# Attention block on one core: reordered first loads, and a reworked last stage

## The chip, the cores and the metric

The kernel runs on one core of one Trainium2 chip. The metric is device time in microseconds (us) of one execution. Each kernel was executed several times; where two kernels are compared, their executions alternated on the same chip. A profile shows one execution; its "span" is about 1.8 us shorter than the time of the same execution (841.5 against 843.27 us for the kernel before).

## The reference, cut to what matters

```python
def setup_inputs():
    B, Sq, D = 8, 208, 1024
    H, Sk, Dh = 32, 1024, 128          # all tensors bf16
    # x (B,Sq,D), k_cache and v_cache (B,H,Sk,Dh), wq (D,H*Dh), wo (H*Dh,D)

def reference(x, k_cache, v_cache, wq, wo):
    q = (x @ wq).reshape(B, Sq, H, Dh).transpose(0, 2, 1, 3)
    scores = einsum("bhqd,bhkd->bhqk", q, k_cache) * (Dh ** -0.5)
    p = softmax(scores, axis=-1)
    o = einsum("bhqk,bhkd->bhqd", p, v_cache)
    return o.transpose(0, 2, 1, 3).reshape(B, Sq, H * Dh) @ wo
```

K and V are 67 MB each and are read once. The weights are 8.4 MB each, x is 3.4 MB.

## The kernel before

The work is cut into 32 blocks: 4 groups of 8 heads, and in each group the 8 batches. A block needs K of its 8 heads (2 MB, transposed on the way in by the DMA), V (two chunks of 1 MB), its group's wq (two halves of 1 MB) and wo (2 MB), and x transposed. TensorE works through the heads one by one: scores, the exponential on ScalarE, the product with V, the row sum, and between them the q projection of a later block and output projections of the block before.

The first loads, in the order in which they are issued (DMAs of `nc.sync` are issued by SyncE, SP in the profile, on its hardware queue; those of `nc.gpsimd` by GpSimd, POOL, on the software queue):

```python
    load_wq_half(0, 0)                                        # POOL, 1 MB
    nc.sync.dma_start_transpose(out=xT[:, :, :Sq], in_=xf[:Sq, :])      # x of batch 0
    ...
    kv_of[0] = load_kv(*blocks[0], first=True)

    def load_kv(g, b, first=False):
        ...
            if first and ck == 0 and hck > 2:                 # K of heads 0 and 1 first, 0.5 MB
                nc.sync.dma_start_transpose(out=kT_c[:, :2 * Sk], in_=k_cache[b, h0:h0 + 2]...)
            else:                                             # K of all 8 heads, 2 MB
                nc.sync.dma_start_transpose(out=kT_c[:], in_=k_cache[b, h0:h0 + hck]...)
        for ck in range(NCKV):                                # two chunks of V
            ...
            nc.sync.dma_start(out=v_c[:], in_=v_cache[...]...)
            if first and ck == 0:
                load_wq_half(g, 1)                            # POOL, 1 MB
                load_wo(g)                                    # POOL, 2 MB
                nc.sync.dma_start_transpose(out=kts[0][:, 2 * Sk:], ...)   # K of heads 2 to 7, 1.5 MB
                nc.sync.dma_start_transpose(out=xT[:, :, Sq:], in_=xf[Sq:, :])  # x of batches 1 to 7, 3 MB
```

The output projection, as the last group runs it. Its one buffer in PSUM, the memory that TensorE writes to, is `po`; VectorE empties it (below called the eviction):

```python
    ps_p = ctx.enter_context(tc.tile_pool(name="f_ps_p", bufs=1, space=PSUM))
    ...
                po = ps_p.tile([128, 512], F32, name="po")
                for hl in range(hg):                          # 8 matmuls of 128x512
                    nc.tensor.matmul(po[...], lhsT=oT[:, hl, r0:r0 + rows], rhs=wo_g[:, hl, ...], ...)
                ...
                    nc.vector.tensor_tensor(out=o_sb[:rows, :], in0=po[:rows, :CW], in1=a, op=ALU.add)
                    nc.vector.reduce_sum(out=fin[...], in_=o_sb[:rows, :], axis=AX.X)
                    nc.sync.dma_start(out=of[...], in_=o_sb[:rows, :])
```

At the end VectorE (DVE) checks sums that were collected (`chk`, `chk_hi`, `fin`) and makes a flag; the flag goes to DRAM by a DMA, every engine loads it into a register, and branches over a slow safe version that is not needed here:

```python
        ...                                                   # 4 compares, 5 reductions, a cast
        nc.tensor.matmul(cnt[0:1, 0:1], lhsT=ok_bf[:], rhs=ones[:], start=True, stop=True)
        nc.vector.tensor_scalar(out=bad[:], in0=cnt[0:1, 0:1], scalar1=127.5, scalar2=None, op0=ALU.is_lt)
        nc.vector.tensor_copy(out=bad_i[:], in_=bad[:])
        nc.sync.dma_start(out=flag_d[:], in_=bad_i[:])
    cond = nc.values_load(flag_d[0:1, 0:1], min_val=0, max_val=1)
    with tc.If(cond > 0):
        mha_slow(tc, x, k_cache, v_cache, wq, wo, out)
```

## Time and profile before

The median was 841.38 us in four runs.

Busy time by stretch, from the windows view of the kernel before. The columns are the stretch in us from the start, its length, the busy time of PE (TensorE matmuls), PEld (weight loads), DVE, ACT and POOL with the number of instructions, the TensorE clock that was granted, the DMA share and the rate in GB/s.

```profile
10.00:20.00 10.00, 4.92 (x31) 3.84 (x29) 1.18 (x2) 0.00 (x0) 0.00 (x0) 0.92 1.08 312
20.00:30.00 10.00, 4.67 (x35) 4.46 (x36) 1.62 (x5) 2.91 (x4) 0.00 (x0) 0.57 1.16 202
30.00:40.00 10.00, 6.76 (x70) 5.98 (x68) 5.37 (x16) 5.52 (x12) 0.00 (x0) 1.00 1.25 236
...
500.00:600.00 100.00, 97.39 (x923) 83.86 (x928) 76.30 (x238) 75.41 (x164) 1.77 (x2) 1.00 0.73 188
```

In the middle (last row) PE is busy 97% of the time and the DMA has room, 0.73. In the head it is the other way round: the DMA is full and PE is half idle.

What PE waited for in the head, from the waits view of the kernel before (engine, tile and line, what it waited for, us in total, times, the longest):

```profile
PE s_ps L316 <- DMA kT_c<-in_k_cache_dram: 14.2, 3, 9.7
PE q L271 <- DMA wq_g<-in_wq_dram: 9.6, 1, 9.6
PE q L271 <- DMA xT_all<-in_x_dram: 3.0, 1, 3.0
```

The three waits for K are those for the heads 0 and 1 (9.7 us, the scores start at 25.3 us), for heads 2 to 7 (2.8 us, at 33.5) and for block 1 (1.6 us, at 58.8).

The DMA view explains the 25.3 us. The first three lines are the stretch from 10 to 18 us, the next three that from 18 to 25 us. GB/s comes in 40 slices; q0 is the software queue (wq half 1 and wo), q1 the hardware queue (here K of heads 0 and 1, by transpose).

```profile
GB/s 175 197 248 390 283 285 283 285 288 421 476 390 326 328 328 376 563 369 306 326 349 398 498 367 305 349 415 480 388 312 324 369 440 476 312 323 317 387 297 337
q0 software_dynamic: 654, 2.58, 82.8%
q1 hardware_dynamic: 911, 0.23, 18.9%
...
GB/s 233 196 197 168 165 165 145 121 117 108 92 80 80 123 67 50 45 45 45 50 48 56 63 51 78 73 60 37 60 37 107 37 48 25 37 48 37 64 138 351
q1 hardware_dynamic: 841, 0.35, 111.4%
q0 software_dynamic: 84, 0.31, 10.8%
```

Until 18 us the software queue moved 2.58 MB and the transpose of K 0.23 MB.

The tail, from the timeline of the kernel before (start, duration, engine, line, operation, tiles, and in brackets the idle time before it and what ended it):

```profile
821.04 0.38 DVE L359 TENSOR_TENSOR oT<-o_ps,rinv 128x208 bf16<-128x208 f32 x1 [0.96 <-ACT rinv L352]
...
822.65 1.89 PE L287 MATMUL po<-wo_g,oT 128*128 128x512 bf16 x8 [0.78 <-DVE o_sb L302]
824.57 0.69 DVE L302 TENSOR_TENSOR o_sb<-po,acc 128x512 bf16<-128x512 f32 x1 [1.26 <-PE po L287]
825.30 0.69 DVE L304 TENSOR_REDUCE fin<-o_sb 128x1 f32<-128x512 bf16 x1
825.32 1.89 PE L287 MATMUL po<-wo_g,oT 128*128 128x512 bf16 x8 [0.78 <-DVE o_sb L302]
...
833.63 0.14 DVE L533 CAST bad_i<-bad 1x1 int32<-1x1 f32 x1
833.84 0.30 SPq L535 DMA_DIRECT2D flag_d<-bad_i  x1
```

The last head is done at 821.4 us. Then PE and DVE take turns at the one PSUM buffer, and the program ends 20.1 us later, at 841.5.

### The profile page before, as it was taken

To read this page: it belongs to the slowest core of one execution; us is meant where nothing else is said; L and a number is where in the kernel's file an instruction comes from. 1 tells how busy PE (TensorE), PEld (TensorE's weight loads), DVE (VectorE), ACT (ScalarE), POOL (GpSimd) and SP (SyncE) were. 2 spreads that over 40 slices of the span, in tenths; PEclk is the share of its full clock that TensorE was granted. 3 is DMA by queue.
4 is the path that set the end of the run, shared out by engine and by line. 5 is a ranking of instruction groups with operands and counts; after the bars stand their busy time and mean duration, and the time that the engine had idled before them with its cause. 6 is when DMAs were issued, how large, how long until landed. Compare 5 with 4: busy or idle time off the path is not lost.

```text
span 841.5 us, 18460 instructions
## 1 busy us (share of the span) xinstructions
PE 776.6 (92%) x7180; PEld 658.5 (78%) x7233; DVE 623.0 (74%) x1889; ACT 590.1 (70%) x1281; POOL 10.9 (1%) x16
## 2 busy tenths in 40 slices
PE   2679999999999999999999999999999999999983
PEld 2578788888878888888788888788888888888861
DVE  0458777778777777777777777777877888888883
ACT  0448677768767778767677877676877867777770
POOL 1000000000000000000000000000000000000000
PEclk9899999999999999999999999999999999999998
DMA  9999686868779787559969957768867986876500
GB/s 239 232 287 230 176 193 162 198 152 241 179 200 249 183 183 197 135 142 248 228 173 226 231 123 193 182 156 238 216 166 230 216 219 166 213 179 175 150 26 29
DMA packets 318497, 159.08 MB, mean 189 GB/s; under 512 B 278210, under 2 KB 281538, under 8 KB 318402
## 3 DMA queue, kind: packets, MB, share of 16 engines
q1 hardware_dynamic: 314114, 141.04, 69.8%
q0 software_dynamic: 4288, 16.78, 6.0%
q8 instruction: 58, 0.95, 0.5%
q14 instruction: 37, 0.30, 0.1%
HBM read 83.89 MB, written 3.41 MB: 104 GB/s over the span
## 4 chain that ended last, share of the span: by engine, by line
PE 51%; DVE 24%; ACT 14%; SPq 5%; issue 3%; DMA 2%; DVEq 0%
PE po L287 21%; DVE t L338 14%; ACT pT L319 13%; PE o_ps L329 11%; PE q L271 10%; PE s_ps L316 9%; DVE oT L359 3%; DVE qT_gb L215 3%; DVE t1c L342 2%; SPq L253 2%; DMA kT_c<-in_k_cache_dram 2%; SPq L255 1%; SPq L240 1%; PE o_ps L348 1%; ACT rinv L352 1%
## 5 line engine op out<-in xcount | busy, mean ns | idle before, releaser
L319 ACT ACTIVATE pT<-s_ps 128x832 bf16<-128x832 f32 x512 | 415.0, 859 | 220.0 <-PE s_ps L316 215.9
L271 PE MATMUL q<-xT_all,wq_g 128*128 128x208 bf16 x2048 | 248.2, 255 | 18.0 <-DMA wq_g<-in_wq_dram 9.6
L316 PE MATMUL s_ps<-qT_gb,kT_c 128*128 128x208 bf16 x2048 | 244.9, 254 | 14.4 <-DMA kT_c<-in_k_cache_dram 14.2
L329 PE MATMUL o_ps<-pT,v_c 128*128 128x208 bf16 x2048 | 241.9, 253 | 14.9 <-DVE oT L359 7.9
L316 PEld LDWEIGHTS <-kT_c 128*128 128x128 bf16 x2048 | 209.6, 144 | 35.1 <-DMA kT_c<-in_k_cache_dram 14.9
L271 PEld LDWEIGHTS <-wq_g 128*128 128x128 bf16 x2048 | 188.9, 99 | 26.5 <-issue 13.3
L329 PEld LDWEIGHTS <-v_c 128*128 128x128 bf16 x2048 | 182.9, 97 | 32.1 <-issue 25.0
L287 PE MATMUL po<-wo_g,oT 128*128 128x512 bf16 x779 | 191.0, 380 | 6.0 <-DVE o_sb L302 2.3
L338 DVE TENSOR_TENSOR t<-pT 128x832 bf16<-128x832 bf16 x256 | 151.6, 592 | 49.3 <-ACT pT L319 36.9
L338 DVE TENSOR_TENSOR t<-t 128x416 bf16<-128x416 bf16 (+1 forms) x512 | 161.8, 316 | 9.0
L342 DVE TENSOR_SCALAR_CACHE_REDUCE t1c<-t 128x208 bf16<-128x208 bf16 x256 | 94.7, 370 | 92.0 <-PE o_ps L348 71.5
L287 PEld LDWEIGHTS <-oT 128*128 128x128 bf16 x832 | 80.3, 98 | 77.3 <-issue 3.2
L352 ACT ACTIVATE rinv<-lnrs 128x208 f32<-128x208 f32 x256 | 97.2, 380 | 7.9
L350 ACT ACTIVATE lnrs<-o_ps 128x208 f32<-128x208 f32 x256 | 89.8, 351 | 2.3 <-PE o_ps L348 2.3
L215 DVE CAST qT_gb<-q 128x416 bf16<-128x416 f32 x128 | 75.1, 587 | 20.5 <-PE q L271 19.9
L359 DVE TENSOR_TENSOR oT<-o_ps,rinv 128x208 bf16<-128x208 f32 (+10 forms) x256 | 83.8, 328 | 2.0 <-ACT rinv L352 1.9
L348 PE MATMUL o_ps<-t1c,ones_bf 128*128 128x208 bf16 x256 | 64.7, 253 | 0.2
L299 DVE TENSOR_TENSOR acc<-po,acc 128x512 f32<-128x512 f32 x52 | 36.0, 692 | 17.1 <-PE po L287 17.1
L352 ACT ACTIVATION_READ_ACCUMULATOR rinv<-lnrs 128x1 f32 x256 | 48.0, 188 | 0.0
L302 DVE TENSOR_TENSOR o_sb<-po,acc 128x512 bf16<-128x512 f32 x26 | 18.0, 691 | 10.2 <-PE po L287 10.2
L348 PEld LDWEIGHTS <-ones_bf 128*128 128x128 bf16 x256 | 25.0, 98 | 0.0
L215 DVE COPY acc<-po 128x512 f32<-128x512 f32 x26 | 18.0, 693 | 8.3 <-PE po L287 8.3
(27 smaller groups left out, 76.5 us busy)
## 6 DMA issues: line engine op xcount, KB each, us to landing
v_c<-in_v_cache_dram SPq DMA_DIRECT2D x64, 1024.0 KB, 5.5
wq_g<-in_wq_dram POOLq DMA_DIRECT2D x8, 1024.0 KB, 8.3
wo_g<-in_wo_dram POOLq DMA_DIRECT2D x4, 2048.0 KB, 10.3
out_dram<-o_sb SPq DMA_DIRECT2D x26, 128.0 KB, 2.1
kT_c<-in_k_cache_dram SPq DMA_TRANSPOSE x33, 11.2
xT_all<-in_x_dram SPq DMA_TRANSPOSE x2, 10.2
flag_d<-bad_i SPq DMA_DIRECT2D x1, 0.0 KB
```

The lines of the kernel that those rows point to most:

```text
L215: nc.vector.tensor_copy(out=out_ap, in_=in_ap)
L271: nc.tensor.matmul(q2[:, j, :Sq], lhsT=wq_h[:, t, hw * 128:(hw + 1) * 128], rhs=xT[:, t, b * Sq:(b + 1) * Sq], start=(t == 0), stop=(t == ...
L287: nc.tensor.matmul(po[:rows, :CW], lhsT=oT[:, hl, r0:r0 + rows], rhs=wo_g[:, hl, c * CW:(c + 1) * CW], start=(hl == 0), stop=(hl == hg - 1))
L316: nc.tensor.matmul(s_ps[:, jj // npb, (jj % npb) * Sq:(jj % npb + 1) * Sq], lhsT=kv[:, t, :], rhs=qT_gb[:, hl, :], start=True, stop=True)
L319: nc.scalar.activation(out=pT[:, half * T2:(half + 1) * T2, :].rearrange("p (a b) s -> p a (b s)", a=2), in_=s_ps[:, :, :npb * Sq], func=A ...
L329: nc.tensor.matmul(o_ps[:, :Sq], lhsT=v_c[:, hh, t, :], rhs=pT[:, t, :], start=(t == 0), stop=(t == T - 1))
L338: nc.vector.tensor_tensor(out=nxt[:], in0=cur[:, :n2, :], in1=cur[:, n2:n, :], op=ALU.add)
L342: nc.vector.tensor_scalar(out=t1c[:], in0=cur, scalar1=T1_CLAMP, scalar2=None, op0=ALU.min, op1=ALU.max, accum_out=chk_hi[:, u["idx"]:u["i ...
L348: nc.tensor.matmul(o_ps[:, 256:256 + Sq], lhsT=ones_bf[:], rhs=u["t1"][:, 0, :], start=True, stop=True)
L350: nc.scalar.activation(out=lnrs[:], in_=o_ps[:, 256:256 + Sq], func=ACT.Ln)
L352: nc.scalar.activation(out=rinv[:], in_=lnrs[:], func=ACT.Exp, scale=-1.0, accum_out=chk[:, u["idx"]:u["idx"] + 1])
L359: nc.vector.tensor_tensor(out=oT[:, u["hl"], c0:c0 + n1], in0=u["o_ps"][:, :n1], in1=u["rinv"][:, :n1], op=ALU.mult)
```

## The change

It shortens the two ends. In the head, what is not needed for block 1's start moves back: x is transposed batch by batch, each a block ahead; wo is cut in halves, half 0 after the first block's V, half 1 after block 1's V; wq half 1 and the first wo halves go through SP instead of POOL. In the tail, the last four output projections take the score tiles' two PSUM buffers; the sum `fin` comes out of the eviction itself; there are fewer checks; and the flag is read from SBUF. Fewer checks also means a weaker one: the two compares of `fin` with a bound became one test that `fin` is finite.

```diff
-    def load_wq_half(g, half):
+    def load_wq_half(g, half, eng=None):
...
-        nc.gpsimd.dma_start(out=w[:], in_=wq[...]...)
+        (eng or nc.gpsimd).dma_start(out=w[:], in_=wq[...]...)
...
+    def load_xT(b0, b1):
+        nc.sync.dma_start_transpose(out=xT[:, :, b0 * Sq:b1 * Sq], in_=xf[b0 * Sq:b1 * Sq, :])
...
+        if g == 0 and not first and b + 1 < B:
+            load_xT(b + 1, b + 2)
         for ck in range(NCKV):
+            if first and ck == 0:
+                load_wq_half(g, 1, eng=nc.sync)
             v_c = ...
             if first and ck == 0:
-                load_wq_half(g, 1)
-                load_wo(g)
                 ... # K of heads 2 to 7
-                    nc.sync.dma_start_transpose(out=xT[:, :, Sq:], in_=xf[Sq:, :])
+                    load_xT(1, 2)
+            if first and ck == NCKV - 1:
+                load_wo(g, 0, eng=nc.sync)
+        if bi == 1:
+            for c in range(1, NC):
+                load_wo(g, c, eng=nc.sync)
...
+                if tail:
+                    po = ps_s.tile([128, 2, 512], F32, name="s_ps")[:, 0, :]
...
-                    nc.vector.tensor_tensor(out=o_sb[:rows, :], in0=po[:rows, :CW], in1=a, op=ALU.add)
-                    nc.vector.reduce_sum(out=fin[...], in_=o_sb[:rows, :], axis=AX.X)
+                        nc.vector.scalar_tensor_tensor(out=o_sb[:rows, :], in0=po[:rows, :CW], scalar=1.0, in1=a,
+                                                       op0=ALU.mult, op1=ALU.add, accum_out=fcol)
...
-        flag_d = dram.tile([1, 1], I32, name="flag_d")
-        nc.sync.dma_start(out=flag_d[:], in_=bad_i[:])
-    cond = nc.values_load(flag_d[0:1, 0:1], min_val=0, max_val=1)
+        cond = nc.values_load(bad_i[0:1, 0:1], min_val=0, max_val=1)
```

Left out: renamings, the checks, and a way to split the last projections by heads that is switched off (`HS = 0`).

## The prediction

> **What bounds the kernel now.** TensorE, except at both ends. In the windows view PE is busy about 97% from 60 to 800 us at granted clock 1.00; one block of eight heads takes about 24.5 us (spacing of the Ln activations in the timeline). The unused time is in the first 60 us (PE busy 31.6, DMA share above 1.0) and after about 813 us.
>
> Head (timeline and landings): K of the first two heads lands at 25.3 us (the scores wait 9.7 us for it), while wq half 1 and the 2 MB wo share the engines; K of heads 2-7 lands at 33.4 (2.8 us of wait), the 3 MB transposed x of batches 1-7 at 45.6 (3.0 us), K of block 1 at 58.75 (1.6 us). The Trainium skill, "DMA: Bandwidth & Descriptors", section "Issuing engines are not separate DMA queues", says that DMAs of all issuers interleave on the same 16 engines; the trace agrees: the software queue's wo landed at 24.9 us and the transpose only then.
>
> Tail: the last oT ends at 821.4; then output projections alternate with the DVE eviction, as there is one PSUM buffer (matmuls 1.9 us, eviction 0.69, PE waits 0.78 each), until 830.6; then fin 0.69, checks to 833.8, the flag's DMA to 834.9, register load 0.66, branch (3.5 us on PE) and end, 841.5.
>
> **What the change does.** Head: block 1's K now stands behind about 9.9 MB instead of 13.4 (six batches of x, wo half 1 and V move behind it). At the 228 GB/s of the old head that is 43 to 45 us. The first K should land near 11 us, heads 2-7 near 25; PE's block 0 work also fits into about 43 us. Against this, x of batch 2 and V of block 1 come after that K, by my estimate 2 to 3 us of new wait near 45-52 us. Net gain 12 us (9 to 14).
>
> Tail: two PSUM buffers and no reduction: the last eviction ends near 826.9 instead of 831.3 on the old clock, 4.4 us. Fewer checks: 0.55 us. The flag read from SBUF: about 1.07 us, its DMA. The branch stays. Last block with 0.69 us less DVE per piece: 0.5 to 1 us, as DVE is 90% busy there. Sum 6.5 to 7 us.
>
> Middle: nothing. The 26 removed reductions (18 us of DVE) are off the critical path: PE's matmuls per 100 us are the same in the last group (902) as in groups without reductions (904, 902). The wo halves and x loads by batch have slack.
>
> **Prediction.** 841.4 - 12 - 7 = 822.4 us, range 816 to 829. Faster by over 2% 0.64, same 0.35, slower 0.01. The 2% line is at 824.6, so the head's size decides.
>
> **What would show each step.** Landings: K of two heads before 13 us, of heads 2-7 at 23-28, of block 1 at 42-47. Ln of block 1's first head near 55 us instead of 67.0. Block length still 24.5 us. In the tail PE runs the last 16 output-projection matmuls almost without waits, no fin reduction, no flag DMA; about 14 us from last oT to the end instead of 20.
>
> **What would make it wrong.** Block 1 waits for x of batch 2 or V longer than 3 us; wq half 1 on SP delays V or K of heads 2-7; early blocks run short of K (new DMA waits at blocks 2 to 4); the eviction with accumulation is much slower than 0.69 us; the register load from SBUF is slower.

## More of the kernel before

Note the granted clock of 0.57 between 20 and 30 us; what PE does do there runs slowly.

From about 19 us on the rate lay between 25 and 123 GB/s for some five microseconds, although the engines were marked busy.

## The result, and the profile after

The changed kernel took 821.78 us (median of 10 runs, 821.08 to 822.73). The ratio to the kernel before is 0.9767, with a 95% interval of 0.9742 to 0.9791. A later set of runs, on another chip, gave 821.07 us and a ratio of 0.9772. The spread fell too: 1.65 us over those 10 runs, against 11 us over the 15 runs of before.

The windows of the changed kernel:

```profile
10.00:20.00 10.00, 7.99 (x76) 7.07 (x75) 4.09 (x10) 3.38 (x5) 0.00 (x0) 1.00 1.11 316
20.00:30.00 10.00, 6.82 (x72) 6.32 (x71) 5.05 (x16) 5.41 (x12) 0.00 (x0) 1.00 1.12 289
30.00:40.00 10.00, 9.68 (x104) 8.97 (x101) 7.07 (x22) 7.86 (x16) 0.00 (x0) 1.00 1.25 244
...
500.00:600.00 100.00, 97.46 (x911) 82.98 (x916) 75.93 (x234) 74.70 (x164) 1.76 (x2) 1.00 0.75 190
```

The DMA is as full as before, but PE gets 72 matmuls instead of 35 between 20 and 30 us, and at full clock. The middle is unchanged.

Its waits in the head. The 8.8 us for x are in truth the start: PE's first matmul needs x of batch 0 and the first half of wq, and both land at about 8.4 us.

```profile
PE q L281 <- DMA xT_all<-in_x_dram: 8.8, 2, 8.6
PE s_ps L335 <- DMA kT_c<-in_k_cache_dram: 2.7, 2, 2.5
PE o_ps L348 <- DMA v_c<-in_v_cache_dram: 1.3, 1, 1.3
PE po L304 <- DMA wo_g<-in_wo_dram: 1.3, 1, 1.3
```

The last line is new: block 1 waits for wo half 1.

The DMA view of 10 to 18 us, to be read beside that of the kernel before: the software queue (q0) is gone from it, and q1 alone moved 2.58 MB (wq half 1, V, then K of heads 2 to 7), where q0 and q1 together had moved 2.81.

```profile
GB/s 133 15 215 256 271 333 343 364 369 369 389 364 374 328 358 379 379 379 389 328 358 410 358 440 358 420 287 348 349 421 273 269 221 288 288 289 292 291 292 289
q1 hardware_dynamic: 3624, 2.58, 106.4%
```

Its tail, by the timeline:

```profile
804.90 0.38 DVE L378 TENSOR_TENSOR oT<-o_ps,rinv 128x208 bf16<-128x208 f32 x1 [1.00 <-ACT rinv L371]
805.76 0.69 DVE L315 SCALAR_TENSOR_TENSOR o_sb<-s_ps,acc 128x512 bf16<-128x512 f32 x1 [0.48 <-PE s_ps L304]
...
806.51 3.61 PE L304 MATMUL s_ps<-wo_g,oT 128*128 128x512 bf16 x16 [0.36 <-DVE o_sb L315]
...
810.16 0.69 DVE L315 SCALAR_TENSOR_TENSOR o_sb<-s_ps,acc 128x512 bf16<-128x512 f32 x1 [1.03 <-PE s_ps L304]
...
812.89 0.15 DVE L555 TENSOR_SCALAR bad_i<-cnt 1x1 int32<-1x1 f32 x1 [0.35 <-PE cnt L550]
```

The last 16 matmuls run as one piece, no separate reduction follows, and the program ends 14.1 us after the last head instead of 20.1.

For the head, three points of the trace say most. They are the starts of PE's scores of head 0, of head 2 and of block 1, with the Ln activation (ScalarE's logarithm of the row sum) of block 1's first head, after which the kernels run alike. In the profiled runs:

| us | scores head 0 | scores head 2 | scores block 1 | Ln block 1 | Ln of last block | last head done | end |
|---|---|---|---|---|---|---|---|
| before | 25.3 | 33.5 | 58.8 | 67.0 | 803.5 | 821.4 | 841.5 |
| after | 13.6 | 23.7 | 40.0 | 49.1 | 787.4 | 805.3 | 819.3 |

So the head gave 17.9 us in this pair, the middle took back 1.8 (738.3 against 736.5 us), the last block stayed at 17.9 us, and the tail gave 6.0. The sum is 22.2 us, 3.7 more than the medians differ (18.5). The profiled run of before took 843.27 us, 3.0 above its median, so its head was one of the slower ones; that is tested next.

### The profile page after: what moved, and what is told of

Its sections match the earlier page's. It is cut to its first block, busy times and chain, and to the rows that moved or that the text cites. A ratio compares the mean times of both kernels' runs of the same rounds, so it can differ in the third digit from the quotient of the medians. Undisturbed runs are those within 1.5% of the kernel's fastest.

```text
span 819.3 us, 18488 instructions
## 1 busy us (share of the span) xinstructions
PE 773.1 (94%) x7181; PEld 655.4 (80%) x7233; DVE 604.6 (74%) x1885; ACT 590.7 (72%) x1281; POOL 11.8 (1%) x17
## 4 chain that ended last, share of the span: by engine, by line
PE 53%; DVE 25%; ACT 14%; DMA 3%; issue 3%; SPq 1%; DVEq 0%
PE po L304 20%; DVE t L357 15%; ACT pT L338 13%; PE o_ps L348 12%; PE q L281 10%; PE s_ps L335 9%; DVE oT L378 4%; DVE qT_gb L215 3%; DVE t1c L361 2%; DMA kT_c<-in_k_cache_dram 2%; DMA wo_g<-in_wo_dram 1%; PE o_ps L367 1%; SPq L243 1%; PE s_ps L304 1%; ACT rinv L371 1%
## 5 line engine op out<-in xcount | busy, mean ns | idle before, releaser
L281 PE MATMUL q<-xT_all,wq_g 128*128 128x208 bf16 x2048 | 245.6, 254 | 14.2 <-DMA xT_all<-in_x_dram 8.8
L335 PEld LDWEIGHTS <-kT_c 128*128 128x128 bf16 x2048 | 208.3, 144 | 23.2 <-DMA kT_c<-in_k_cache_dram 3.2
L348 PEld LDWEIGHTS <-v_c 128*128 128x128 bf16 x2048 | 182.8, 97 | 33.1 <-issue 23.7
L304 PE MATMUL po<-wo_g,oT 128*128 128x512 bf16 x749 | 183.1, 380 | 4.0 <-DMA wo_g<-in_wo_dram 1.3
L380 DVE TENSOR_TENSOR oT<-o_ps,rinv 128x192 bf16<-128x192 f32 (+9 forms) x80 | 21.8, 273 | 0.0
```

The costliest lines, as they stand in the source:

```text
L281: nc.tensor.matmul(q2[:, j, :Sq], lhsT=wq_h[:, t, hw * 128:(hw + 1) * 128], rhs=xT[:, t, b * Sq:(b + 1) * Sq], start=(t == 0), stop=(t == ...
L304: nc.tensor.matmul(po[:rows, :CW], lhsT=oT[:, hl, r0:r0 + rows], rhs=wo_g[:, hl, :], start=(i == 0), stop=(i == len(heads) - 1))
L335: nc.tensor.matmul(s_ps[:, jj // npb, (jj % npb) * Sq:(jj % npb + 1) * Sq], lhsT=kv[:, t, :], rhs=qT_gb[:, hl, :], start=True, stop=True)
L348: nc.tensor.matmul(o_ps[:, :Sq], lhsT=v_c[:, hh, t, :], rhs=pT[:, t, :], start=(t == 0), stop=(t == T - 1))
```

## The experiments

All outputs are right. "Old" and "new" below are the two kernels. There were three sets of runs, each on one chip; the old kernel's median in them was 839.10, 840.67 and 840.08 us.

### The old kernel once more

No edit.

> The kernel before, once more: the noise, and the head of another execution. In the tail-only run, whose head is the same program, block 1's K landed at 55.6 and the Ln of block 1's first head came at 63.8 us; in the profiled run of before at 58.75 and 67.0. If the profiled run of before had an unlucky head, this one shows K at 54 to 56, Ln at 62 to 64, a span of 836 to 838 and the same tail of 20.1 us; then the head's gain is 13 to 14 us, not 17.9. If it shows 58 to 59 and 67 again, the gain is 17.9 and something else lengthens the changed kernel in its other runs.

Measured: 839.64 us, ratio 0.9994 (0.9946 to 1.0043). Its profiled run had a span of 840.3 us, with block 1's K at 57.7 us and the Ln at 66.0. This is neither of the two answers expected. Three profiles of the same head (before, this one, and the tail-only run below) have the Ln at 67.0, 66.0 and 63.8 us, and their slow DMA stretch lasts until 24.9, 23.9 and 21.6 us, which is when wo lands. From that Ln to the Ln of the last block they agree within 0.13 us. So nearly the whole spread between these three profiles is made in the head. For a run of median length I estimate the Ln at 64.0 us: 840.28, less 1.8 for the difference of time and span, less the 774.5 us that follow the Ln in the profile.

### The two parts alone

The head-only kernel is the new one with the old output projection, checks and flag; the tail-only kernel is the old one with the new ones:

```diff
# tail only: the old loads, with
-        for p in oproj_pieces(gl, j):
+        for p in oproj_pieces(gl, j, mode="final", tail=True):
# head only: the new loads, with the old oproj_pieces and the old checks and flag
```

> Head of the change alone, tail of before. If the two parts add, with the spans of the two profiles split at the Ln of block 1's first head (67.0 before, 49.1 after) and at the last oT: block 1's K lands at 40 us as in the changed kernel (39.98), the Ln comes at 49, and the time is the changed kernel's plus 6.1 us of tail: about 828. Rival: part of the gain of 18.5 us between the medians comes from the removed reductions in the last group; then the time is above 829.

> Tail of the change alone, head of before. Additive theory: 6.1 us less than before (840.3 median), so about 834; from the last oT to the end 14.0 us instead of 20.1, and the same distance from the Ln of the last block's first head to the last oT (17.9 us). Rival, the step of the prediction that the reductions cost the last block 0.5 to 1 us: that distance falls below 17.4 us.

Measured: head only 827.01 us, ratio 0.9853 (0.9837 to 0.9870); tail only 834.91 us, ratio 0.9951 (0.9935 to 0.9968). The old kernel beside them took 839.10.

Head only is 12.1 us below the old kernel by the medians, with block 1's K at 40.6 us and the Ln at 49.7. That is the prediction's 12. Tail only is 4.2 us below, where 6.1 were expected. Its profile shows the full tail gain: 13.9 us from the last head to the end, and 768.3 us from the Ln of block 1 to the end against 774.5. So the rest is missing before that Ln, in the varying head that it shares with the old kernel. Whether its unprofiled runs had slower heads wasn't seen. The last block took 17.85 us (old: 17.89), so the removed reductions gave that block nothing: the prediction's 0.5 to 1 us for it is wrong, and the rival with it.

### What makes the head shorter: the queue, or the bytes ahead

The queue-only kernel changes nothing but the issuer. Back-on-POOL undoes just that in the new kernel:

```diff
# queue only, on the old kernel
-                load_wq_half(g, 1)
-                load_wo(g)
+                load_wq_half(g, 1, eng=nc.sync)
+                load_wo(g, eng=nc.sync)
# back on POOL, on the new kernel
-                load_wq_half(g, 1, eng=nc.sync)
+                load_wq_half(g, 1)
-                load_wo(g, 0, eng=nc.sync)
+                load_wo(g, 0)
```

> Before, but wq half 1 and the whole wo are issued on SP, in their old place; the same 13.4 MB stand ahead of block 1's K. Theory A, the prediction's (only the bytes ahead count): block 1's K lands at 57 to 59 us (58.75 before), Ln of block 1's first head at 66 to 67, time 839 to 841. Theory B (4 KB packets of the software queue alternate with the transpose's 256-byte packets and leave engines straggling at 35 to 117 GB/s from 18.8 to 24.6 us): the first K lands at 9 to 11 instead of 25.3 us, the slow stretch goes, block 1's K lands at 53 to 55, time 834 to 836.

> The changed kernel with wq half 1 and wo half 0 issued on POOL again; the same bytes in all ahead of block 1's K. Theory A: block 1's K at 39 to 41, time 821 to 823 as the changed kernel. Theory B: the first K lands at 18 to 21 us instead of 10.0, a slow stretch returns, block 1's K lands at 43 to 46 us, time 825 to 827.

Measured: queue only 838.37 us, ratio 0.9993 (0.9977 to 1.0010): no gain. Back on POOL 828.12 us, ratio 0.9866 (0.9850 to 0.9883): 6.3 us above the new kernel's 821.78. (The new kernel did not run in this set; by the two ratios, 0.9866 and 0.9767, it is about 8 us.) The same switch is worth nothing clear of noise in one surrounding and 6 us or more in the other, so neither theory as written was enough.

The landings do follow theory B. In queue only the first K landed at 10.1 us and block 1's K at 53.6. In back-on-POOL they landed at 20.6 and 45.1 us, against 10.0 and 40.0 in the new kernel, with the same bytes ahead. The packet records of back-on-POOL show how. Packets started in each 2 us, by queue and size; q1 is the transpose of K (256-byte packets) until V follows (2048 bytes):

```
10.0 228GB/s q1/256B x114 25ns; q0/4096B x104 206ns; q0/4B x6 11ns
12.0 359GB/s q1/256B x199 21ns; q0/4096B x163 185ns; q0/4B x7 12ns
14.0 264GB/s q1/256B x354 46ns; q0/4096B x107 184ns; q0/4B x9 10ns
16.0 150GB/s q1/256B x371 85ns; q0/4096B x50 184ns; q0/4B x8 11ns
18.0 94GB/s q1/256B x642 62ns; q0/4096B x6 184ns; q0/4B x2 12ns; q1/4B x2 9ns
20.0 381GB/s q1/2048B x368 90ns; q1/256B x30 18ns; q1/4B x30 9ns
```

Alone, the transpose starts 2266 such packets in 2 us (290 GB/s; the new kernel, 18 to 20 us). Next to the software queue it starts 114 and 199 in the first two rows, about one for each packet of 4096 bytes, and more as those thin out. In the old kernel, from 10 to 16 us, it is 513 to 481. The Trainium skill, "DMA: Bandwidth & Descriptors", section "Queues, rings and completion order", says that each DMA engine goes round-robin between the queues at packet granularity. These counts agree: one small packet in turn with one large one, while both queues are full. In effect the software queue's 3 MB in the old kernel go ahead of K, wherever the program issues them. Then comes a slow stretch (16 to 20 us here), in which the rate is 94 to 150 GB/s and a 256-byte packet takes 62 to 85 ns on the mean instead of 18. This is the part that the bytes don't tell. Its cause is not shown: the packet records name no engine. Nor is it peculiar to the software queue. The new kernel has two shorter ones, from 21.5 and from 37.9 us, each after a packet of 16 KB that fetched instructions (last section); they delay the same two loads of K.

Why, then, did queue only gain nothing? In it PE's waits for K of heads 2 to 7 (5.1 us) and for wq (the second 3.4) took the place of the first wait. With wq half 1 and wo in one line before K of heads 2 to 7, that K landed at 30.0 us, hardly earlier than in the tail-only run's old head (30.5). Its profiled run was also the fastest of its four, 1.6 us below their median, so its row in the table below flatters it.

### Which part of the new order counts

x by batch only, on the old kernel, and the same together with the queue:

```diff
# x by batch, on the old kernel; the second kernel also has the queue-only edit
+        if g == 0 and not first and b + 1 < B:
+            load_xT(b + 1, b + 2)
...
-                    nc.sync.dma_start_transpose(out=xT[:, :, Sq:], in_=xf[Sq:, :])
+                    load_xT(1, 2)
```

> Before with x transposed batch by batch only: 10.9 MB instead of 13.4 MB ahead of block 1's K, wq half 1 and wo still on the software queue. If bytes ahead count (2.55 MB at about 250 GB/s), block 1's K lands 10 us earlier than in before's usual runs, at 44 to 47 us, and the time is 829 to 831. If the software queue's slow stretches decide, not the bytes, K lands at 50 us or later and the time is above 833.

> Before, with wq half 1 and the whole wo on SP as in the queue-only run, and x batch by batch as in the x-only run; wo is not deferred. Block 1's K should land at 43 to 44 us (10.9 MB at 250 GB/s), K of heads 2-7 at 30 as in the queue-only run. If block 1's K decides, the Ln of block 1's first head follows it by 9 us, at 52 to 53, and the time is 828 to 829.5 (tail of before, 6 us, included). If K of heads 2-7 decides (25.4 us from its landing to that Ln in the changed kernel, 28 with a cold clock), the Ln comes at 55.5 to 58 and the time is 832 to 834.

Measured: x by batch 834.13 us, ratio 0.9923 (0.9873 to 0.9972). Block 1's K landed at 46.5 us as the bytes said, but the time was 3 us above the expected. With the queue as well 831.22 us, ratio 0.9893 (0.9863 to 0.9923), K at 45.4, between the two expectations.

Here are the three points of the trace for the heads in question. "Old tail" marks kernels that still have the 6 us of the old tail. The points are those of one profiled run each, and that run was not always near the median: before was 3.0 us above it, x by batch 2.4 above, queue only 1.6 below, the others within 0.8.

| us | scores head 0 | scores head 2 | scores block 1 | from head 2 to block 1 | block 1's K landed | median time |
|---|---|---|---|---|---|---|
| before (old tail) | 25.3 | 33.5 | 58.8 | 25.3 | 58.8 | 840.28 |
| queue only (old tail) | 13.5 | 30.1 | 53.6 | 23.5 | 53.6 | 838.37 |
| x by batch (old tail) | 23.6 | 31.8 | 50.6 | 18.8 | 46.5 | 834.13 |
| queue and x (old tail) | 14.1 | 29.5 | 45.9 | 16.4 | 45.4 | 831.22 |
| head only (old tail) | 13.6 | 23.6 | 40.6 | 17.0 | 40.6 | 827.01 |
| back on POOL (new tail) | 20.7 | 29.2 | 47.8 | 18.6 | 45.1 | 828.12 |
| after (new tail) | 13.6 | 23.7 | 40.0 | 16.3 | 40.0 | 821.78 |

There are two gates. The first is K of heads 2 to 7; from its landing on PE needs about 16.3 us for what is left of block 0. The second is block 1's K with x of batch 1. Where the last column but one is well below the start of block 1's scores (x by batch, back on POOL), the second gate stood open and PE was still busy. Splitting x opens the second gate: the stretch falls from 25.3 to 18.8 us, and 6.5 us is also what this kernel gained by the medians of its set (840.67 less 834.13). The rest, from 31.8 to 23.7 us for head 2, is the first gate, and it needs both the order (wo behind that K, 29.5 to 23.6 us from "queue and x" to "head only") and the queue (without it wq half 1 and wo go in front again, 29.2 us in "back on POOL"). That is why the queue alone showed nothing.

The stretches of 18.6 and 18.8 us, against 16.3, go with a lower clock. From the windows view, x by batch and then back on POOL:

```profile
20.00:30.00 10.00, 6.19 (x40) 5.55 (x40) 2.34 (x7) 3.35 (x4) 0.00 (x0) 0.57 1.19 245
30.00:40.00 10.00, 8.12 (x70) 7.64 (x71) 4.93 (x16) 4.88 (x11) 0.00 (x0) 0.83 1.14 226
...
20.00:30.00 10.00, 6.83 (x45) 6.23 (x46) 3.26 (x9) 3.35 (x4) 0.00 (x0) 0.67 1.18 302
30.00:40.00 10.00, 9.94 (x98) 9.55 (x97) 5.82 (x19) 7.30 (x15) 0.00 (x0) 0.88 1.14 194
```

Both had let PE wait for the first K, 8.1 and 4.3 us, and were granted 0.57 to 0.88 afterwards, where the new kernel was granted 1.00. The Trainium skill, "TensorE: Matmul & The Clock Gate", section "Part 1: The HAM clock gate", says that an idle window of about 3.4 us puts the array to half clock; these windows agree. That the clock makes the whole difference of 2.3 to 2.5 us is not shown: no run changed the clock alone ("queue and x" was granted 0.82 and 0.84 and still took 16.4, having less left to do at head 2).

### The tail's one buffer

The new kernel, with the last four projections in the old single PSUM buffer:

```diff
-        for p in oproj_pieces(gl, j, mode="final", tail=True):
+        for p in oproj_pieces(gl, j, mode="final"):
```

> The changed kernel, but the last four output projections go through the one PSUM buffer of the others again; fused eviction and short flag path stay. If the two buffers are most of the 4.2 us that the evictions gained, each of the last three projections waits for the eviction before it (0.7 us) and none starts before the last oT: the last eviction ends 9.0 to 9.2 us after the last oT instead of 5.6, and the time is 3.0 to 3.6 us above the changed kernel run beside it. Rival: the removed reduction was what the last stage waited for; then it is under 1 us.

Measured: 824.95 us, ratio 0.9817 (0.9787 to 0.9847); the new kernel beside it 821.07, so 3.9 us. By its timeline:

```profile
806.75 1.89 PE L304 MATMUL po<-wo_g,oT 128*128 128x512 bf16 x8 [0.79 <-DVE o_sb L315]
808.68 0.69 DVE L315 SCALAR_TENSOR_TENSOR o_sb<-po,acc 128x512 bf16<-128x512 f32 x1 [1.98 <-PE po L304]
809.43 1.89 PE L304 MATMUL po<-wo_g,oT 128*128 128x512 bf16 x8 [0.79 <-DVE o_sb L315]
```

The turns are back, with 0.79 us of wait for each eviction, although no reduction follows any more. From the last head to the end it takes 17.9 us instead of 14.1 to 14.4. So the second buffer was worth 3.5 to 3.9 us. The separate reduction was worth about its own 0.7 us at the very end: DVE is done with it 9.9 us after the last head in the old kernel, and with the last eviction after 9.2 us here.

### Is the middle bound by TensorE?

A head with an output projection costs PE about 3.9 us, one without 2.2, while ScalarE needs 2.64 us a head if the durations of its instructions are added up. (They overlap: its busy time in the page of the kernel before is 590.1 us for 256 heads, 2.3 us each.) The pieces come in the first heads of a block; this kernel spreads them evenly:

```diff
-            ofill.run(max(1, tail_rate[0]))
+            credit[0] += credit[1]              # pieces of the block / 8 heads
+            n_run = int(credit[0] + 1e-6)
+            credit[0] -= n_run
+            ofill.run(n_run)
```

> The changed kernel, and the output projection's pieces of a block spread evenly over its eight heads instead of one per head from the first on. A head with a piece takes 3.9 us of matmuls, one without 2.2, but ScalarE needs 2.64 us a head. If heads without a piece wait for ScalarE (theory: the middle is bound in turn by TensorE and by ScalarE), a block falls from 24.5 us to 23.4-24.1 and the time to 800-812. If TensorE is the bound all along (what the prediction said), the time stays within 819 to 823.

Measured: 822.05 us, ratio 0.9787 (0.9740 to 0.9835). The theory fell. By the spacing of the Ln (medians), heads without a piece took 2.25 us instead of 2.46, and those with one 4.26 instead of 3.96: what the ones gained the others lost. The middle is bound by PE, as the prediction said.

### Repairs

First, wo half 1 ahead of block 1's second V chunk, and the checks of `chk` and `chk_hi` ahead of the last evictions:

```diff
             vs.append(v_c)
+            if bi == 1 and ck == 0:
+                for c in range(1, NC):
+                    load_wo(g, c, eng=nc.sync)
...
+            if j == NTT - 1 and pre_last is not None:
+                pre_last()                      # the two checks, in place on chk and chk_hi
```

> The changed kernel with two repairs: wo half 1 is issued ahead of the second V chunk of block 1 (block 1 took 24.1 us instead of 22.7, with 1.3 us of wait for wo), and the two checks of chk run where DVE waits, ahead of the last evictions. If the wait is the new cost, block 1 takes 22.7 to 23 us again; the checks save 0.9 to 1.1 us from the last eviction to the flag. Time 819 to 820.5. If V then comes late instead, block 1 keeps its 24 us.

Measured: 819.88 us (819.65 to 820.52), ratio 0.9764 (0.9717 to 0.9811). Block 1 took 22.8 us (24.1 in the new kernel's first profile, 23.2 in its second, 22.7 in the old kernel), and no wait for wo is left. The tail took 12.97 us instead of 14.07. This version is the fastest. It ran on another chip than the new kernel's runs, so the 1.2 to 1.9 us between their medians stand on the two named differences of the profiles, not on the ratio. (In its own set the spread kernel, otherwise the new one, took 822.05 us.)

Then a bolder one on top of it: K of heads 2 to 7 in two parts, both halves of wo behind block 1's K, block 1's projections later:

```diff
+                    for h1, h2 in ((2, 4), (4, hck)):
+                        nc.sync.dma_start_transpose(out=kts[0][:, h1 * Sk:h2 * Sk], ...)
...
-            if first and ck == NCKV - 1:
-                load_wo(g, 0, eng=nc.sync)
+            if bi == 1:
+                load_wo(g, ck, eng=nc.sync)
```

> The repaired kernel (wo half 1 early, checks early), with K of heads 2-7 loaded as heads 2-3 and 4-7, both halves of wo behind block 1's K, and block 1's two pieces of output projection at its fourth and sixth head. 8.9 MB ahead of block 1's K. If the head is bound by these bytes and by K of heads 2-7, the wait of 2.5 us for it goes, block 1's K lands at 36 to 37.5 us, the Ln of block 1's first head comes at 45.5 to 47.5, and the time is 816 to 818. If V of block 1 or wo then come late, the waits for them return 2 us or more and the time stays at 819 to 820.

Measured: 823.6 us (821.89 to 825.36), ratio 0.9798 (0.9762 to 0.9834): slower than the repair, and than the new kernel beside it (821.07). The head did get shorter, with the scores of head 2 at 19.3 us and the Ln at 47.5, but block 1 then took 30.2 us. Its waits between 60 and 75 us:

```profile
PE o_ps L346 <- DMA v_c<-in_v_cache_dram: 3.7, 1, 3.7
PE q L279 <- DVE t L355: 0.6, 1, 0.6
```

V of block 2 landed at 70.8 us. Up to there the DMA had no pause, so the earlier start of block 1 was lost again, in part to a wait for block 2's load. That wait is 3.7 of the 7.4 us by which this block 1 is longer than the repair's 22.8. The rest is not taken apart by a run; after the wait the granted clock was 0.83 (70 to 80 us).

### The new kernel once more

No edit; this run stood beside the one-buffer kernel, the bolder repair and "queue and x".

> The changed kernel once more, beside these runs on the same chip: 821 to 822.7, K of heads 2-7 at 23 to 25, block 1's K at 39.5 to 41.5, Ln of block 1's first head at 49 to 50.5.

Measured: 821.07 us (820.45 to 821.79), ratio 0.9772 (0.9742 to 0.9803). In its profile K of heads 2 to 7 landed at 23.5 us, block 1's K at 39.9, the Ln came at 49.8, block 1 took 23.2 us and the tail 14.4. So the new head comes out nearly the same each time, where the old one's Ln lay between 63.8 and 67.0 us.

## Why the prediction was right

The time, 821.8 us, is 0.6 us from the forecast 822.4. A match that close is partly luck. The Ln came 5.9 us earlier than forecast (49.1 instead of 55), but 3.0 of this only make up for the slow head of the profiled run of before (67.0 against the estimated 64.0), and 1.8 were given back in the middle. Point by point:

- **What bounds the kernel** held: the middle is PE's (the spread pieces changed nothing), the ends are not.
- **Head, 12 us.** Head only gave 12.1 us by the medians. For the new kernel the estimated usual Ln of before (64.0 us) less 49.1 gives about 15, of which 1.8 were given back. The size is right, but the reasoning behind it is only part of the truth. "43 to 45 us" at 228 GB/s, and with it the Ln "near 55 us", was too late: K landed at 40.0 us and the Ln came at 49.1. That is 9.9 MB at 247 GB/s. The old rate contained the slow stretch behind the software queue: by the packet records, up to the landing of block 1's K, the two kernels with the loads on POOL moved 244 (old) and 231 GB/s (back on POOL), those with them on SP 264 (queue only) and 263 (new). (V, which the forecast counts among what moves behind that K, did not move: the 3.5 MB less are six batches of x and wo half 1.) And the bytes ahead of block 1's K are not the only gate: with the same bytes, back on POOL was 6.3 us slower. "PE's block 0 work also fits" was the second half of the answer, since PE was ready only because K of heads 2 to 7 came at 23.7.
- **"2 to 3 us of new wait" for x of batch 2 and V of block 1** did not come: 0.2 us for that x, none for V. In their place block 1 waited 1.3 us for wo half 1. The sentence "The wo halves and x loads by batch have slack" is the step that failed, for wo half 1; the prediction gives no number for it.
- **Tail, 6.5 to 7 us**, was 6.0: evictions 4.2 (forecast 4.4), checks 0.4 (0.55), flag 1.10 (1.07), the shorter register load and the rest 0.3 (not forecast), last block 0.0 (forecast 0.5 to 1). Two buffers as its main cause are shown by the one-buffer run.
- **Middle, nothing**: apart from block 1 the blocks agree to 0.4 us in sum. The 18 us of DVE work that went from the last group changed no time.

What stays open: head only and tail only add to 16.3 us by the medians, the whole change to 18.5 and 19.0 in its own two sets. The old head varies by some microseconds from run to run, which is enough for it, but it isn't shown run by run. What makes the slow stretches slow is open too.

## What to carry to other kernels

Ask of each load at the start which first use of PE it delays, and count what is ahead of that load on every queue: here a plain load on the software queue passed a transpose that was issued before it (wo landed at 24.9 us, K at 25.3), so a load isn't out of the way because it is on another queue. A change of queue was worth nothing clear of noise under the old order and 6 us or more under the new one, so test such changes in both surroundings. Where the DMA is full, shortening one wait moves it to the next load in line; look a block further before you call it gained.

## What the Trainium skill lacked or had wrong

- "DMA: Bandwidth & Descriptors", section "Rules for kernel authors", says that spreading DMAs over the issuers doesn't help bandwidth. It lacks that it can starve a transpose: beside the software queue's 4096-byte packets, the transpose's 256-byte packets came at 152 to 185 in 2 us (old kernel, 10 to 16 us) instead of 2266, K landed at 25.3 instead of about 10 us, and moving two loads to the software queue cost the new kernel 6.3 us.
- No page that I read has the stretch that follows: rates of 25 to 123 GB/s for some 5 us with the engines marked busy, of varying length, in heads where the old kernel's runs differ by several us.
- "DMA: Bandwidth & Descriptors", section "Latency and other measured facts", gives about 350 to 400 GB/s for contiguous DMA transposes (261 for a non-contiguous middle dimension). The plateau here was 290 GB/s, and K of one block lies in one piece in DRAM.
- The same section gives about 600 ns as the floor of a register load. From DRAM it took 0.66 us here, from SBUF 0.47 us.
- No page that I read has what becomes of a transpose in flight at an instruction fetch (one packet of 16 KB on queue 8). At 21.5 us in the new kernel it took 1.1 us, 256-byte packets after it took up to 1.4 us instead of 18 ns, and the rate fell from 285 to 87 GB/s for the next two microseconds. It is no single case: in the 14 traces there are 203 such fetches while a transpose alone was moving, at a median of 289 GB/s, and the median over the next two microseconds (0.2 to 2.0 us after the start of the fetch) is 72. In 212 stretches of transpose in the new kernel without a fetch near it is 290.
